# Weaving VectorE's score matmuls into ScalarE's units, with 69 instead of 74 quads on VectorE

## The chip, the cores and the metric

The kernel runs on one core of a Trainium2 chip. The metric is the device time of one execution in microseconds; lower is better. The core's engines work from their own instruction queues, in order, and wait for one another by semaphores: TensorE (PE in the profile: matrix products into PSUM, eight banks of 128 x 512 fp32), ScalarE (ACT), VectorE (DVE), GpSimd (POOL) and SyncE (SP, which mainly issues DMAs).

## The reference

One transformer block on 2048 tokens of width 640, in bf16: layer norm, attention with 32 heads of 20, a residual, a second layer norm, a gated FFN of width 1728 with the tanh Gelu, a residual. Cut to what is computed:

```python
q, k, v = split((layernorm(x) @ wqkv).reshape(B, S, 3, 32, 20))
scores  = einsum("bhqd,bhkd->bhqk", q, k) * 20 ** -0.5
o       = einsum("bhqk,bhkd->bhqd", softmax(scores), v)
h       = x + o.reshape(B, S, 640) @ wo
n       = layernorm(h)
out     = h + (gelu(n @ w_gate) * (n @ w_up)) @ w_down
```

The scores are 32 x 2048 x 2048, 134 million exponentials; they are what the kernel spends its time around.

## The kernel before

**Chunks and slots.** The queries go in eight chunks (`SIZES`, L320: 512, five of 256, two of 128). A chunk has as many slots as it takes to go through the eight groups of four heads, with 512 score columns a slot per key row: 32 slots in all. In a slot the keys are walked in key blocks of 128. A *tile* is one head's 128 x 512 scores: one matmul of 512 columns, or two of 256, or four of 128, one for each of its key blocks. A head's 20 rows sit in one of four groups of 32 rows of TensorE (`tile_position=(32 * j, 0)`, L969), so the matmuls of four different heads can run side by side. A *quad* is the four heads' tiles of one place: 16 quads a slot, 512 in all, 2048 tiles.

**Two engines take exponentials.** ScalarE takes most tiles, in *units* of three or two tiles, on PSUM banks 0 to 2 and 3 to 4 by turns, with one activation a unit that reads 1536 or 1024 columns and writes bf16 probabilities into a ring of 18 tiles (`pts` with 12 and a part of `rege` with 6, `PR, PR2`, L339). VectorE takes the quads that `D_QUADS` (L340) counts for each slot, 74 in all, with a polynomial: an eviction from PSUM to int16 for each tile (L893), then a chain of six elementwise steps for two or four tiles together, in some slots with a DMA that adds in place. `D_PART` (L341) says within what part of a slot those tiles are placed in the slots that have no lead (`lead`, L820); in the others they run ahead of their slot.

**Where VectorE's tile is issued.** At most one tile of VectorE goes with a unit (`dtile`). In slots 8 to 11 (`SIX`) it takes the unit's third bank and is part of the unit's matmuls. Elsewhere it is an operation of its own, tagged SD (L992), on a bank that is neither of the two unit sets (7, 5 or 4), priority 1, and may start once its own unit's matmuls are issued (`after=[qk]`). `fit` (L838) picks one whose row group its unit does not use.

**Sums.** Probabilities times values (`pv_op`, L926) run with four heads in four column groups into bank 6, two quads at a time in strict order; a VectorE quad is summed by itself, and the last sum of a slot stands behind all of VectorE's quads of that slot. Then VectorE copies bank 6 to `osb` (L1051), TensorE transposes it, VectorE divides. A unit's activation cannot write its ring place before the sum that read it has run.

**FFN.** When a chunk's slots are done, `post` (L1087) does output projection, residual, layer norm, gate (L1142), Gelu (in place, up to 2048 columns at once, on ScalarE), up, product (L1191) and `down` (L1222), as background between the next chunks' scores. The last chunk's has nothing left to lie behind. Each change between exponential, Gelu and square root needs a table load on ScalarE.

**The order** is not written by hand. `Sched.schedule` (L94) simulates the engines with constants for each operation's duration and picks, at each moment and engine, the ready operation of the best priority whose PSUM banks are free; TensorE's operations have a mode (row for scores, col for sums, full), and one of the current mode is preferred among the low priorities. Where TensorE would idle it inserts matmuls that compute nothing of use (`warm`, `pad`). `emit` then writes each engine's queue in the order found, with waits derived from the dependencies; on the chip the order is fixed and only the times differ. All of an operation's waits stand ahead of its first instruction, but for dependencies of TensorE on itself. Operations recorded through the helper `I` show L372 whatever they are.

Of the kernel before, what the change touches and what calls it, by code (L numbers as in the profile page):

```python
# [16 lines left out]
SEM_ANY = 0.036  # L17
# [3 lines left out]
QK_LEAD = .65  # L21
PE_AGE = 1.5
SD_ALONE = .21
P_SD = 1
LNB = 2

MODE_SWITCH = {"pe": .098, "act": 1.44}
# [19 lines left out]
class Sched:  # L47
# [3 lines left out]
    def __init__(self, nc):  # L51
        self.nc = nc
        self.ops = []
        self.lw = {}
        self.rd = {}
        self.warm = None
        self.pad = None
        self.left = {}
        self.ev = 9

    def op(self, eng, fns, dur, prio, reads=(), writes=(), acq=(), rel=(), after=(), sem=None, lat=None, mode=None, util=0.0):
        if eng == "dve" and rel and prio > self.ev:
            prio = self.ev
        o = Op()
        o.i = len(self.ops)
        o.eng, o.dur, o.lat, o.sem = eng, dur, DRAIN[eng] if lat is None else lat, sem
        o.util = util
        o.mode = mode
        o.tag = writes[0] if writes else None
        o.fns = fns if isinstance(fns, list) else [fns]  # L70
        o.prio = (prio, o.i)
        deps = set(after)
        for r in reads:
            if r in self.lw:
                deps.add(self.lw[r])
        for w in writes:
            if w in self.lw:
                deps.add(self.lw[w])
            deps.update(self.rd.get(w, ()))
        for r in reads:  # L80
            self.rd.setdefault(r, []).append(o.i)
        for w in writes:
            self.lw[w] = o.i
            self.rd[w] = []
        deps.discard(o.i)
        o.deps = deps
        o.acq = list(acq)
        o.rel = list(rel)
        o.succ = []
        o.ready = 0.0  # L90
        self.ops.append(o)
        return o.i

    def schedule(self):  # L94
        ops = self.ops
# [22 lines left out]
        while done < total:  # L118
# [4 lines left out]
            for e in ENGINES:  # L123
# [4 lines left out]
                    continue  # L128
                skipped = []
                kept = set()  # L130
                chosen = None
                while ready[e]:
                    p, i = heapq.heappop(ready[e])
                    o = ops[i]
                    got = []
                    if e == "pe" and due is not None and o.prio[0] > 0 and t < due < t + o.dur + (MODE_SWITCH[e] if mode[e] not in (None, o.mode) else 0):
                        skipped.append((p, i))
                        if len(skipped) >= 60:
                            break
                        continue  # L140
                    for bk in o.acq:
                        for b in bk.allowed:
                            if owner[b] is None and free_at[b] <= t + 1e-9 and b not in got and b not in kept:
                                got.append(b)
                                break
                        else:
                            got = None
                            break
                    if got is None:

                        if p[0] == 0:
                            kept.update(bk.allowed[0] for bk in o.acq)
                        skipped.append((p, i))
                        continue
                    skipped.append((p, i))
                    if chosen is None:
                        chosen, banks = o, got
                        if e != "pe" or p[0] < 1 or o.mode == mode[e] or t - o.ready > PE_AGE:
                            break
                    elif o.mode == mode[e]:  # L160
                        chosen, banks = o, got
                        break
                    if len(skipped) >= 60:
                        break
# [34 lines left out]
                    if chosen is None:  # L199
                        continue  # L200
                o = chosen
                if e == "pe" and o.tag and o.tag[0] == "S":
                    self.spare = self.spares[o.tag[1]]
                if e == "pe" and self.pad is not None and o.tag and o.tag[0] in ("O", "OD"):
                    s_ = o.tag[1] if o.tag[0] == "O" else o.tag[1][0]
                    self.left[s_] -= 1
                    live, begun = self.left[s_] > 0, True
                    while recent and recent[0][0] < t - PAD_WIN:
                        recent.popleft()
                    u = sum(x for _, x in recent) + o.util  # L210
                    room = due - t - MODE_SWITCH[e] if due is not None and due > t else 1e9
                    while u < PAD_MIN * PAD_WIN and o.util < 1.1 and o.dur + 0.215 < room and (live or o.tag[0] == "O"):
                        o.fns = o.fns + self.pad
                        o.dur += 0.215
                        o.util += 0.213
                        u += 0.213
                o.start = t
                if e == "act":
                    due = t + o.dur + (0.905 if o.dur > 1.2 else 1.332) - QK_LEAD if o.mode == "exp" else None
                if o.util:  # L220
                    recent.append((t, o.util))
                if o.mode is not None:
                    if o.tag and o.tag[0] == "SD" and (mode[e] != "row" or t - free[e] > 0.06):
                        o.dur = SD_ALONE
                    if mode[e] not in (None, o.mode):
                        o.dur += MODE_SWITCH[e]
                    mode[e] = o.mode
                free[e] = t + o.dur
                o.fin = t + o.dur + o.lat
                heapq.heappush(events, free[e])  # L230
                for bk in o.rel:
                    b = bk.b
                    owner[b] = None
                    free_at[b] = o.fin + SEM_LAT.get((e, "pe"), SEM_ANY)
                    last[b] = o.i
                    heapq.heappush(events, free_at[b])
                for s in o.succ:
                    q = ops[s]
                    q.ready = max(q.ready, free[e] if q.eng == e == "pe" else o.fin + SEM_LAT.get((e, q.eng), SEM_ANY))
                    q.nd -= 1  # L240
                    if q.nd == 0:
                        heapq.heappush(future[q.eng], (q.ready, q.prio, q.i))
                        heapq.heappush(events, q.ready)
                order.append(o)
                done += 1
        self.order = order
        self.span = max(o.fin for o in ops)

# [88 lines left out]
DA_ISSUE, DA_LAT = 0.95, 7.0  # L337
DA_SLOTS = (1, 2, 3, 5) + tuple(range(9, 32))
PR, PR2 = 12, 6  # L339
D_QUADS = (1,) + (2,) * 11 + (2, 3, 2, 3, 2, 2) + (3, 3, 2) * 3 + (3, 3, 2, 3, 2)  # L340
D_FIRST, D_PART = 2, 0.65  # L341
D_LEAD = ((0,) * 8, (0, 10, 20) + (36,) * 21)
D_WIDE = 18
RSQRT_MAGIC = float(0x5F3759DF)
# [6 lines left out]
def bass_sequential_preLN__mha_block__glu_gated_geglu__prompt_kernel(  # L351
# [12 lines left out]
    with ExitStack() as es:  # L364
# [120 lines left out]
        def bank(b, n=512):  # L485
            return PS[:, 512 * b.b:512 * b.b + n]
# [377 lines left out]
        d_ops = []  # L864
        exp_ops = []
        p_next = [0]

        def q_done(k):
            return sum((tuple(last_qk[c]) for c, (q0, _) in enumerate(CHUNKS) if q0 // 512 == k), ())
# [75 lines left out]
        def unit(u):  # L945
# [19 lines left out]
            def qk_mms(out, x, kk):  # L965
                s_, g, kb, j = x
                q0, nq = CHUNKS[slots[s_][0]]
                kt = kb * (512 // nq) + kk
                return lambda eng: eng.matmul(out()[:, kk * nq:(kk + 1) * nq],  # L969
                                              kt_all[32 * j:32 * j + 32, g, kt * 128:(kt + 1) * 128],  # L970
                                              qt_all[32 * j:32 * j + 32, q0 // 512, g, q0 % 512:q0 % 512 + nq],
                                              start=True, stop=True, tile_position=(32 * j, 0), skip_group_check=True)
# [7 lines left out]
            for kk in range(nkm):  # L980
                for i, x in enumerate(al):
                    if kk < 512 // CHUNKS[slots[x[0]][0]][1]:
                        fns.append(qk_mms(lambda i=i: PS[:, 512 * (s0 + i):512 * (s0 + i) + 512], x, kk))
                        reads += qk_reads(x)
            qk = op("pe", fns, 0.222, P_QK, mode="row", util=0.0533 * len(al), reads=reads, writes=[("S", u), "qkseq"] + ([("SD", xd)] if six else []), acq=bks)
            for x in al:
                last_qk[slots[x[0]][0]].append(qk)
            if six:
                bd = bks[2]
            elif xd:  # L990
                bd = Bank(*BG[tl[0][0]])
                qd = op("pe", [qk_mms(lambda: bank(bd), xd, kk) for kk in range(512 // CHUNKS[slots[xd[0]][0]][1])],  # L992
                        0.21 if xd[3] in [x[3] for x in tl] else 0.01,
                        P_SD, mode="row", util=0.0533, reads=qk_reads(xd), writes=[("SD", xd)], acq=[bd], after=[qk])
                last_qk[slots[xd[0]][0]].append(qd)
            n = 512 * na
            pk = [("P", p0 + i) for i in range(na)]
# [320 lines left out]
```

## Time and profile before

| | us |
|---|---|
| median of 3 runs | 911.2 (911.09 to 912.03) |
| the profiled execution, whole | 910.3 |
| its span, first to last instruction | 908.4 |
| first exponential starts, last one ends | 33.6, 877.3 |
| ScalarE busy from 33.6 to 877.3 | 833.1 of 843.7 |
| TensorE busy in the same stretch | 785.0 of 843.7 |
| VectorE busy in the same stretch | 727.4 of 843.7 |
| TensorE busy from 877.3 to the end | 27.6 of 31.1 |

The granted TensorE clock is full throughout. An engine's busy time is the union of its instructions' times, and two neighbouring activations overlap in the trace by some 0.2 us, so ScalarE looks busy even where one starts late: lateness has to be read from the distance of starts. In the timeline, neighbours of one kind are merged into one line: start, time from the first's start to the last's end, engine, line, shape and count, and in brackets the idle time before and what ended it.

### The profile page before, as it was taken

How to read it: one execution, taken by the hardware profiler on the slowest of the kernel's cores; microseconds unless marked ns; L12 is line 12 of the kernel's file. 1: busy time of each engine (PE TensorE's matmuls, PEld its weight loads, DVE VectorE, ACT ScalarE, POOL GpSimd, SP SyncE). 2: the span in 40 equal slices, each digit the busy share in tenths (PEclk: the TensorE clock that was granted, in tenths of full speed). 3: DMA queues.
4: the chain of work that ended last, by engine and by line, in shares of the span. 5: the costliest groups of instructions: out<-in, count | busy, mean ns of one | idle time of the engine just before them, and what ended most of it. 6: DMA issues, size and time to landing. Idle time of an engine off the chain costs nothing.

```text
span 908.4 us, 25274 instructions
## 1 busy us (share of the span) xinstructions
PE 831.5 (92%) x11183; PEld 386.0 (42%) x11228; DVE 768.4 (85%) x1445; ACT 867.3 (95%) x782; POOL 133.3 (15%) x242
## 2 busy tenths in 40 slices
PE   3999999998898887889999999999999998999998
PEld 1432232222233332334444445444444445656777
DVE  8869889988798985899987996899899889889743
ACT  7999899999999999999999999999999999999972
POOL 5001110010013110112313010021012101201200
PEclk9999999999999999999999999999999999999999
DMA  7213334344603322234444232424342343434200
GB/s 260 85 31 82 74 79 113 87 108 96 243 1 65 60 48 35 37 59 81 82 98 58 49 71 48 77 63 86 77 86 51 60 97 57 58 78 94 57 9 23
DMA packets 52933, 68.59 MB, mean 76 GB/s; under 512 B 20940, under 2 KB 38440, under 8 KB 52824
## 3 DMA queue, kind: packets, MB, share of 16 engines
q0 software_dynamic: 13392, 34.08, 20.7%
q1 hardware_dynamic: 39432, 32.89, 13.6%
q8 instruction: 88, 1.44, 0.7%
q14 instruction: 21, 0.17, 0.1%
HBM read 20.12 MB, written 8.09 MB: 31 GB/s over the span
## 4 chain that ended last, share of the span: by engine, by line
ACT 55%; PE 28%; DVE 14%; POOL 3%; issue 1%; DVEq 0%
ACT pts L372 34%; ACT rege L372 19%; PE ps L969 8%; PE ps L372 5%; PE ps L671 5%; PE ps L1142 5%; PE ps L1222 4%; DVE dwx L372 3%; DVE qt_all L372 2%; DVE rege L893 1%; DVE qt_all L893 1%; POOL nw L372 1%; DVE rege L1109 1%; ACT L372 1%; DVE stats L372 1%
## 5 line engine op out<-in xcount | busy, mean ns | idle before, releaser
L372 ACT ACTIVATE pts<-ps 128x1024 bf16<-128x1024 f32 (+1 forms) x467 | 552.9, 1330 | 7.0 <-PE ps L372 5.5
L969 PE MATMUL ps<-qt_all,kt_all 32*128 32x256 bf16 (+2 forms) x4096 | 314.2, 272 | 39.6 <-ACT pts L372 19.2
L372 ACT ACTIVATE rege<-ps 128x1024 bf16<-128x1024 f32 (+1 forms) x231 | 284.5, 1328 | 3.5 <-PE ps L372 3.1
L969 PEld LDWEIGHTS ps<-qt_all,kt_all 32*128 32x128 bf16 x4096 | 108.7, 92 | 246.2 <-ACT pts L372 124.5
L1142 PE MATMUL ps<-rege,regw 128*128 128x256 bf16 (+2 forms) x1101 | 154.5, 272 | 8.8 <-DVE rege L1191 3.6
L372 PE MATMUL ps<-pts,v_all 128*21 128x256 bf16 (+2 forms) x2330 | 122.0, 275 | 0.6 <-ACT rege L372 0.5
L1142 PEld LDWEIGHTS ps<-rege,regw 128*128 128x128 bf16 x1120 | 86.2, 98 | 59.0 <-issue 25.2
L893 DVE TENSOR_SCALAR rege<-ps 128x512 int16<-128x512 f32 x124 | 84.8, 686 | 15.6 <-PE ps L969 14.9
L372 PE MATMUL ps<-rege,v_all 128*21 128x256 bf16 (+2 forms) x1358 | 91.8, 279 | 0.7 <-DVE osb L372 0.4
L671 PE MATMUL ps<-regw 128*128 128x512 bf16 (+1 forms) x344 | 84.1, 354 | 4.7 <-ACT regw L619 1.8
L893 DVE TENSOR_SCALAR qt_all<-ps 128x512 int16<-128x512 f32 x116 | 79.4, 686 | 9.7 <-PE ps L969 8.2
L1222 PE MATMUL ps<-regw,rege 128*128 128x320 bf16 x448 | 77.6, 301 | 1.6 <-DVE rege L1226 0.5
L372 DVE TENSOR_TENSOR qt_all<-qt_all 128x1024 int16<-128x1024 f16 (+3 forms) x81 | 74.7, 922 | 1.1
L372 PEld LDWEIGHTS ps<-pts,v_all 128*21 128x21 bf16 x2330 | 53.6, 91 | 30.6 <-issue 25.0
L372 DVE TENSOR_SCALAR qt_all<-qt_all 128x2048 int16<-128x2048 int16 (+3 forms) x112 | 63.0, 566 | 0.9
L372 PE MATMUL ps<-kt_all,zer 128*32 128x512 bf16 x620 | 54.8, 386 | 0.3 <-DVE osb L372 0.3
L1191 DVE TENSOR_TENSOR rege<-rege,ps 128x512 bf16<-128x512 bf16 (+1 forms) x53 | 35.9, 679 | 21.4 <-PE ps L1142 21.0
L372 DVE TENSOR_SCALAR rege<-rege 128x1024 int16<-128x1024 int16 (+2 forms) x114 | 48.5, 439 | 5.4 <-DMA rege<-qt_all 4.3
L372 DVE TENSOR_TENSOR rege<-rege 128x1024 f16<-128x1024 f16 (+1 forms) x74 | 50.5, 683 | 0.8
L1222 PEld LDWEIGHTS ps<-regw,rege 128*128 128x128 bf16 x448 | 37.6, 98 | 28.9 <-issue 12.3
L671 PEld LDWEIGHTS ps<-regw 128*128 128x128 bf16 x360 | 28.8, 99 | 47.7 <-issue 23.8
L372 POOL DMA_DIRECT2D qt_all<-dwx x25 | 23.0, 921 | 169.2 <-DVE dwx L372 158.6
(114 smaller groups left out, 802.0 us busy)
## 6 DMA issues: line engine op xcount, KB each, us to landing
qt_all<-dwx POOLq DMA_DIRECT2D x19, 512.0 KB, 4.7
rege<-rege POOLq DMA_DIRECT2D x16, 256.0 KB, 3.6
rege<-qt_all POOLq DMA_DIRECT2D x8, 512.0 KB, 4.9
dvx<-qt_all POOLq DMA_DIRECT2D x7, 512.0 KB, 4.7
rege<-in_A_x_dram SPq DMA_DIRECT2D x5, 640.0 KB, 5.7
q_rows<-regw SPq DMA_DIRECT2D x20, 128.0 KB, 1.8
out_dram<-rege SPq DMA_DIRECT2D x16, 160.0 KB, 3.2
regw<-in_B_w_gate_dram SPq DMA_DIRECT2D x1, 2160.0 KB, 12.4
```

Source lines behind the costliest of these rows:

```text
L372: return lambda eng: getattr(eng, method)(*args, **kwargs)
L671: yield op("pe", lambda eng, l=l, r=r, k=k: eng.matmul(bank(bk, n), l, r, start=(k == 0), stop=(k == len(steps) - 1)), c_mm(n) + cold, pri ...
L893: d_ops.append(op("dve", lambda eng: eng.tensor_scalar(v[:, 512 * h:512 * h + 512], bank(b), EXP_MUL, -32000.0, ALU.mult, ALU.max), c_dve( ...
L969: return lambda eng: eng.matmul(out()[:, kk * nq:(kk + 1) * nq], kt_all[32 * j:32 * j + 32, g, kt * 128:(kt + 1) * 128], qt_all[32 * j:32 ...
L1109: op("dve", lambda eng, bk=bk, tt=tt, hf=hf, i=i: eng.tensor_tensor(h_sb[:, tt, hf * 320:(hf + 1) * 320], bank(bk, 320), h_sb[:, tt, hf * ...
L1142: op("pe", lambda eng, a=a, f=f, fi=fi: eng.matmul(bank(bk)[:, fi * nq:(fi + 1) * nq], w[:, a, F0[f]:F0[f] + 128], hnT[:, a, 128 * tb:128 ...
L1191: hdone.append(op("dve", lambda eng, bu=bu, fv=fv, w=w: eng.tensor_tensor(fv, fv, bank(bu, w), ALU.mult), c_dve(w), p, reads=[ku] + hkeys( ...
L1222: op("pe", lambda eng, f=f, o=o, hf=hf, bk=bk: eng.matmul(bank(bk, 320), ha_f[:, o:o + 128], wd[:, f, hf * 320:(hf + 1) * 320], start=(f = ...
```

## The change

Four parts. First, `JOIN`: when the planner picks a unit's score operation, it looks among the ready VectorE tiles for one whose row group the unit does not use, with as many key blocks, whose bank is free now or within 0.2 us, and which belongs to this unit or one already issued. If there is one, its matmuls are woven between the unit's, key block by key block; the unit's operation takes over its waits, and only the last matmul of the tile stays behind as the tile's own operation. The planner's start of the unit moves to when that bank is free. Second, a VectorE tile becomes ready with the unit ahead of its own (`after=[prev]`), but is held until its own unit is issued or takes it along. Third, `D_QUADS` sums to 69 instead of 74: one more in slots 12 to 17, three fewer in 18 to 26, three fewer in 27 to 31. Fourth, `D_PART` goes from 0.65 to 0.55. An SD operation that is not woven in is always counted with `SD_ALONE`.

```diff
+JOIN = 0.2
...
+                    if i in self.small and not hasattr(ops[self.small[i][2]], "start"):
+                        skipped.append((p, i))
+                        if len(skipped) >= 60:
+                            break
+                        continue
...
                 o = chosen
-                if e == "pe" and o.tag and o.tag[0] == "S":
+                t0 = t
+                if o.i in self.heads:
                     self.spare = self.spares[o.tag[1]]
+                    js, nk = self.heads[o.i]
+                    for x in sorted(x for x in ready[e] if x[1] in self.small):
+                        j, nk_, own = self.small[x[1]]
+                        q = ops[x[1]]
+                        b = next((b for b in q.acq[0].allowed if owner[b] is None and free_at[b] <= t + JOIN and b not in banks), None)
+                        if nk_ != nk or j in js or b is None or not (own == o.i or hasattr(ops[own], "start")):
+                            continue
+                        ready[e].remove(x)
+                        heapq.heapify(ready[e])
+                        q.acq[0].b = b
+                        owner[b] = q.acq[0]
+                        if last[b] is not None:
+                            q.deps = set(q.deps) | {last[b]}
+                        q.deps = set(q.deps)
+                        o.deps = set(o.deps) | (q.deps - {o.i})
+                        n = len(o.fns) // nk
+                        o.fns = sum((o.fns[n * k:n * k + n] + q.fns[k:k + 1] for k in range(nk)), [])[:-1]
+                        q.fns = q.fns[-1:]
+                        q.dur = 0.01
+                        join = q
+                        t0 = max(t, free_at[b])
+                        break
...
-                o.start = t
...
+                for o in ([o, join] if join is not None else [o]):
+                    o.start = t0 if o is chosen else free[e]
...
-                    if o.tag and o.tag[0] == "SD" and (mode[e] != "row" or t - free[e] > 0.06):
-                        o.dur = SD_ALONE
...
-D_QUADS = (1,) + (2,) * 11 + (2, 3, 2, 3, 2, 2) + (3, 3, 2) * 3 + (3, 3, 2, 3, 2)
-D_FIRST, D_PART = 2, 0.65
+D_QUADS = (1,) + (2,) * 11 + (3, 2) * 3 + (2, 2, 3) * 3 + (2,) * 5
+D_FIRST, D_PART = 2, 0.55
...
+            prev = s_last[0]
+            s_last[0] = qk
+            if not six:
+                sc.heads[qk] = (set(x[3] for x in tl), nkm) if len(set(CHUNKS[slots[x[0]][0]][1] for x in tl)) == 1 else ((0, 1, 2, 3), 0)
...
-                qd = op("pe", [qk_mms(lambda: bank(bd), xd, kk) for kk in range(512 // CHUNKS[slots[xd[0]][0]][1])],
-                        0.21 if xd[3] in [x[3] for x in tl] else 0.01,
-                        P_SD, mode="row", util=0.0533, reads=qk_reads(xd), writes=[("SD", xd)], acq=[bd], after=[qk])
+                nd = 512 // CHUNKS[slots[xd[0]][0]][1]
+                qd = op("pe", [qk_mms(lambda: bank(bd), xd, kk) for kk in range(nd)], SD_ALONE,
+                        P_SD, mode="row", util=0.0533, reads=qk_reads(xd), writes=[("SD", xd)], acq=[bd], after=[prev] if prev is not None else [])
+                sc.small[qd] = (xd[3], nd, qk)
```

More of the change, by code (lines that the diff above doesn't have):

```diff
@@ L58, in __init__ @@
         self.left = {}
+        self.heads = {}
+        self.small = {}
         self.ev = 9
@@ L130, in schedule @@
                 kept = set()
+                join = None
                 chosen = None
@@ L216, in schedule @@
                         u += 0.213
-                o.start = t
[L218 to L222, printed above, removed]
-                    if o.tag and o.tag[0] == "SD" and (mode[e] != "row" or t - free[e] > 0.06):
-                        o.dur = SD_ALONE
-                    if mode[e] not in (None, o.mode):
-                        o.dur += MODE_SWITCH[e]
-                    mode[e] = o.mode
@@ L228, in schedule @@
[L228 to L243, printed above, removed]
@@ L244, in schedule @@
-                order.append(o)
-                done += 1
+                for o in ([o, join] if join is not None else [o]):
+                    o.start = t0 if o is chosen else free[e]
+                    if e == "act":
+                        due = t + o.dur + (0.905 if o.dur > 1.2 else 1.332) - QK_LEAD if o.mode == "exp" else None
+                    if o.util:
+                        recent.append((t, o.util))
+                    if o.mode is not None:
+                        if mode[e] not in (None, o.mode):
+                            o.dur += MODE_SWITCH[e]
+                        mode[e] = o.mode
+                    free[e] = o.start + o.dur
+                    o.fin = o.start + o.dur + o.lat
+                    heapq.heappush(events, free[e])
+                    for bk in o.rel:
+                        b = bk.b
+                        owner[b] = None
+                        free_at[b] = o.fin + SEM_LAT.get((e, "pe"), SEM_ANY)
+                        last[b] = o.i
+                        heapq.heappush(events, free_at[b])
+                    for s in o.succ:
+                        q = ops[s]
+                        q.ready = max(q.ready, free[e] if q.eng == e == "pe" else o.fin + SEM_LAT.get((e, q.eng), SEM_ANY))
+                        q.nd -= 1
+                        if q.nd == 0:
+                            heapq.heappush(future[q.eng], (q.ready, q.prio, q.i))
+                            heapq.heappush(events, q.ready)
+                    order.append(o)
+                    done += 1
@@ L866, in bass_sequential_preLN__mha_block__glu_gated_geglu__prompt_kernel @@
         p_next = [0]
+        s_last = [None]
         def q_done(k):
```

## The prediction

> **What bounds the kernel now.** I read the totals of the page first, then ScalarE's instructions kept apart by shape.
>
> ```profile
> span 908.4 us, 25274 instructions
> PE 831.5 (92%) x11183; PEld 386.0 (42%) x11228; DVE 768.4 (85%) x1445; ACT 867.3 (95%) x782; POOL 133.3 (15%) x242
> ...
> L372 ACT ACTIVATE pts<-ps 128x1536 bf16<-128x1536 f32 x237 | 360.3, 1540 | 3.5 <-PE ps L372 2.2 <-PE ps L969 0.9
> L372 ACT ACTIVATE pts<-ps 128x1024 bf16<-128x1024 f32 x230 | 254.3, 1113 | 3.5 <-PE ps L372 3.3 <-PE ps L969 0.2
> L372 ACT ACTIVATE rege<-ps 128x1536 bf16<-128x1536 f32 x119 | 181.2, 1533 | 3.2 <-PE ps L372 2.9 <-PE ps L969 0.2
> L372 ACT ACTIVATE rege<-ps 128x1024 bf16<-128x1024 f32 x112 | 124.0, 1112 | 0.3 <-PE ps L372 0.3
> ```
>
> ScalarE (ACT) is the engine to watch: 698 exponentials, 356 of three tiles (1536 columns) and 342 of two (1024), with hardly any idle time before them. But neighbours overlap at their ends, so durations mislead and starts must be read. In the timeline of ScalarE alone:
>
> ```profile
> 403.45 2.49 ACT L372 ACTIVATE rege<-ps 128x1536 bf16<-128x1536 f32 x2
> 405.68 4.78 ACT L372 ACTIVATE pts<-ps 128x1536 bf16<-128x1536 f32 x4
> 410.15 2.57 ACT L372 ACTIVATE rege<-ps 128x1536 bf16<-128x1536 f32 x2
> 412.38 4.86 ACT L372 ACTIVATE pts<-ps 128x1536 bf16<-128x1536 f32 x4
> ```
>
> Four of them (two pairs) take 405.68 to 410.15, 4.47 us; a pair (five tiles) takes 2.23. Taken one by one, the usual distance to the next start is 1.330 after a three-tile one and 0.903 after a two-tile one. That floor is 356 x 1.330 + 342 x 0.903 = 782.3 us. The first starts at 33.6, the last ends at 877.3: 843.7 us, so 61.4 are something else: 37 for the Gelus inside that stretch with their table loads (the rows of 128x2048, x1536, x1792 and x1024 give 25.0, ten loads of 1.28 give 12.8, less overlap), and about 24 of lateness. Of the lateness, nine places where the exponential waits for a sum (matmuls of pts or rege with v_all) hold 10.7 us, fifty places where it waits for its own scores (L969) hold 8.9, the rest is scatter below 0.06 each. After 877.3 the chain of waits runs on TensorE (PE) almost without a break for 31.1 us: left-over FFN work and the last chunk. So the time is: 33.6, then the exponentials' floor, the Gelus, the lateness, then a TensorE tail.
>
> **How a VectorE score tile is priced today.** The score matmuls of TensorE, four lines of its timeline:
>
> ```profile
> 385.70 0.40 PE L969 MATMUL ps<-qt_all,kt_all 32*128 32x256 bf16 x6
> ...
> 387.05 0.41 PE L969 MATMUL ps<-qt_all,kt_all 32*128 32x256 bf16 x8
> ...
> 387.94 0.39 PE L969 MATMUL ps<-qt_all,kt_all 32*128 32x256 bf16 x4
> ...
> 403.69 0.61 PE L969 MATMUL ps<-qt_all,kt_all 32*128 32x256 bf16 x8
> ```
>
> x4 is a unit of two tiles, x6 at 385.70 two tiles with a VectorE tile behind them, x8 at 387.05 three with one behind: 0.39, 0.40, 0.41. A tile that follows its own unit already runs beside it, in the free 32-row group. Only where the row group is taken, or the tile stands by another unit, does it cost more (403.69: +0.22). In the built order 126 of the 259 tiles with an operation of their own follow their unit at once; 133 do not. So "issued among them" cannot save for the first half.
>
> **The change, part by part.**
> 1. *Fewer quads on VectorE.* D_QUADS sums to 69 after 74: 20 tiles move to ScalarE, and the built program has 358 three-tile and 349 two-tile exponentials: 2 x 1.330 + 7 x 0.903 = **+9.0 us**, all on ScalarE's path. Nothing hides it. VectorE, the engine that gains (20 evictions of 0.69 and five polynomial chains, some 36 us in all), was not the bound.
> 2. *Joined score matmuls.* 135 of 236 tiles are now woven in (123 into their own unit); 101 still stand apart. Counting VectorE tiles as 0.01 behind or in their own unit and 0.21 elsewhere, they cost TensorE 29.2 us before and 19.6 after. But there are nine more units (0.22 each) and 50 more changes between row, column and full mode, of about 0.11 each (PV at 403.14, sixteen matmuls worth 0.43, next scores at 403.69), +5.5. With every operation of the two built orders at the chain's prices (0.22 for a unit or a quad's sum, 0.056, 0.11 and 0.136 for full matmuls of 128, 256 and 320 columns), TensorE's work adds up to 800.5 before and 799.6 after. TensorE is not relieved. The late scores need the PE at the right moment, not less work: I give them -1.0 (bounds -5, if most of 8.9 goes, to +1).
> 3. *A wait placed in front.* A woven unit must hold VectorE's bank as well as its own before its first matmul; 107 score operations now carry a separate VectorE wait, after 30, and PE waits of this sort last 51 ns each in the trace. Before, a late VectorE stood behind the unit:
>
> ```profile
> 582.17 0.39 PE L969 MATMUL ps<-qt_all,kt_all 32*128 32x256 bf16 x2 [0.48 <-DVE rege L893]
> ```
>
> Of 153 groups with a free row group, 40 waited 0.05 to 0.85 us there, 7.6 us in all, and it hurt no exponential, whose scores were already out. Now it would: queued behind such a wait are the unit's scores, then the sums and FFN matmuls. 53 joins are with three-tile units, whose scores have only some 0.2 us of slack (start at +0.45 after the preceding two-tile exponential's start is the last that showed no lateness); with two-tile units there is 0.4 more. 53 x 40/153 x 0.19 is 2.6; with part absorbed by slack and part of the 51 ns added, **+2.3** (bounds 0 and 135 x 0.2 = 27, the planner's whole allowance; nearest to the row above, so near the low end).
> 4. *VectorE tiles earlier in a slot (0.55).* The nine waits for sums come from the ring of 18 probability tiles:
>
> ```profile
> 97.25 1.45 ACT L372 ACTIVATE rege<-ps 128x1536 bf16<-128x1536 f32 x1 [2.70 <-PE ps L372]
> ```
>
> At a slot's end its last sum waits for VectorE's tiles of that slot, the ring stays full, ScalarE waits. In the built order these are the places where a unit's ring space is freed by a sum that TensorE issues after that unit's scores: nine such before, the nine found in the trace, five after. A place with nothing but the sum between cost 0.38 to 0.69 (mean 0.56), one with another unit between 1.29 to 2.92. After: two of the first kind, three of the second (2.0, 2.5 and 1.3 by likeness): 6.9 instead of 10.7, **-3.8** (bounds -8 and 0).
> 5. *The end.* After the last scores 51 fewer down matmuls (320 columns, 0.136 each by the chain) and 36 more gate/up ones (0.056) are left, but one Gelu of 1792 columns, before ahead of the last exponentials, now stands behind them, between two more table loads. ScalarE's path before that point loses 1.68. In the tail:
>
> ```profile
> 877.33 1.28 ACT L372 ACT_TABLE_LOAD   x1
> 878.62 0.20 ACT L372 ACTIVATE nm<-off 128x1 f32<-128x1 f32 x1
> 881.27 0.70 ACT L619 ACTIVATE rege<-ps 128x640 bf16<-128x640 bf16 x1 [2.44 <-PE ps L613]
> ```
>
> The copy at 881.27 (3.94 behind the last exponential) comes at 1.28 + 0.20 + 1.28 + 1.68 = 4.44: 0.5 later. The second new load falls in the 4.23 idle before the square root. From the copy: output projection 1.36, then 59 ups and 23 downs 6.4 (before: 4.0), second transposes and copy 1.2, 140 gate/ups 7.8, VectorE 0.5, 28 downs 4.0, add and store 2.8: 29.4 against 31.1, **-1.7** (bounds -3.5, +2.5). Gelu and tail together -3.4.
>
> The trace has a Gelu starting 1.30 us after its load does (857.51, 858.81), so 1.28 is a load's whole price. ScalarE: Activation LUTs in the Trainium skill, section What ACT_TABLE_LOAD costs, adds a drain of 1.38 us, 2.66 in all; by it the copy would come 2.8 us later still and the sum would be +5.9. The trace disagrees, so it gets no chance of its own.
>
> **Sum.** 9.0 - 1.0 + 2.3 - 3.8 - 3.4 = +3.1 us against the profiled execution (span 908.4, 910.3 as a whole). The median of the runs shown is 0.9 above it, 911.2, and goes with it: **914.3**.
>
> **Rivals.** About 0.2% (1.8 us) is what a measurement here can tell from no change.
> - *Lateness nearly gone, faster.* The woven order removes both kinds: ring -7, scores -5, no new waits: 9.0 - 12 - 3.4 = -6.4, 904.8. For it: VectorE has 36 us less to do, and over-full pairs of units (more PE work between scores than the exponentials last) fall from 244 to 220. Against: PE work is the same, and five ring places are visible in the order. Chance 0.27.
> - *VectorE in front of the scores, much slower.* If half of the 135 joined units wait 0.2 and the slack is already used up by PE being busy, +10 in place of 2.3, about 922. It decides from a mean of some 0.15 us in three-tile units. For: VectorE's 85% and the 40 waits above. Against: VectorE gets lighter. Chance 0.15. In TensorE: Matmul & The Clock Gate of the Trainium skill, section The mechanism, matmuls start and end strictly in program order; that is the rule that lets one bank hold up a unit, and the line at 582.17, where the sums stood behind it, agrees.
> - *It does nothing that matters:* weaving saves nothing as half ran side by side, and ring and tail pay for the nine units: -1 to +1, 911.3. Chance 0.13.
> - *Forecast:* 0.45, its own range 912 to 918.
>
> Faster 0.28, same 0.14, slower 0.58. The range 904.5 to 921 holds the forecast, the small case, most of the faster one and half of the slower.
>
> **What would show it.** ScalarE: 707 exponentials at the same 1.330 and 0.903; lateness by sums near 7 us at five places; the last Gelu behind the last exponential, with the tail near 29.4. TensorE: 4 tiles in 0.41, more VectorE releases ahead of L1001. I am wrong if lateness falls below 13 us in all (faster), or if waits for scores rise far above 10 us.

## The result, and the profile after

The changed kernel takes 914.5 us (median of 12 runs, 911.3 to 915.9), the kernel before 911.1 on the same chip (median of 12): a ratio of 1.0034, 95% interval 1.0024 to 1.0045. It is slower by 3.4 us. The totals of its page:

```profile
span 912.2 us, 25442 instructions
PE 840.6 (92%) x11261; PEld 380.1 (42%) x11261; DVE 739.8 (81%) x1405; ACT 876.6 (96%) x793; POOL 125.1 (14%) x238
```

And ScalarE's exponentials apart by shape (busy time and mean; then idle time before them, by what ended it):

```profile
L403 ACT ACTIVATE pts<-ps 128x1536 bf16<-128x1536 f32 x238 | 378.9, 1607 | 6.8 <-PE ps L403 3.7 <-PE ps L1001 3.0
L403 ACT ACTIVATE pts<-ps 128x1024 bf16<-128x1024 f32 x236 | 276.1, 1186 | 0.1
L403 ACT ACTIVATE rege<-ps 128x1536 bf16<-128x1536 f32 x120 | 192.3, 1612 | 3.7 <-PE ps L403 2.2 <-PE ps L1001 1.5
L403 ACT ACTIVATE rege<-ps 128x1024 bf16<-128x1024 f32 x113 | 134.4, 1192 | 0.0
```

VectorE fell from 768.4 to 739.8 us of work, ScalarE rose from 867.3 to 876.6, and there are 707 exponentials in place of 698. The span is best taken apart along ScalarE, with the starts: the first exponential, then all exponentials at 1.330 and 0.903 us each (the floor), then what the distances between neighbouring exponentials exceed that (lateness, by what was waited for; the rest is scatter below 0.06 each), then everything else up to the table load behind the last exponential (Gelus, loads), then the tail. The same sum for every kernel of this study, each from its own profiled execution, in us:

| | span | first | floor | late: sums | late: scores | scatter | Gelus, loads | tail |
|---|---|---|---|---|---|---|---|---|
| before | 908.4 | 33.6 | 782.3 | 10.7 (9 places) | 8.8 | 2.8 | 39.0 | 31.0 |
| after | 912.2 | 32.9 | 791.3 | 7.0 (5) | 9.5 | 3.4 | 37.9 | 30.4 |
| e1, quads alone | 913.0 | 33.8 | 791.3 | 7.0 (6) | 9.6 | 3.3 | 37.5 | 30.4 |
| e2, 0.55 alone | 903.4 | 33.5 | 782.3 | 6.2 (7) | 8.3 | 3.0 | 39.0 | 31.1 |
| e3, both numbers | 910.5 | 33.6 | 791.3 | 2.6 (4) | 11.9 | 3.3 | 37.4 | 30.5 |
| e4, tile behind | 913.4 | 33.6 | 791.3 | 7.0 (5) | 9.2 | 4.1 | 37.8 | 30.3 |
| e5, transposes 4.0 | 907.2 | 32.7 | 791.3 | 6.8 (5) | 4.7 | 3.5 | 37.8 | 30.3 |
| e6, no weaving | 913.8 | 32.4 | 791.3 | 7.2 (5) | 4.6 | 3.4 | 37.7 | 37.3 |
| e7, 0.50 alone | 908.8 | 33.1 | 782.3 | 6.1 (6) | 14.1 | 3.3 | 38.9 | 31.0 |
| e8, price 0.21 | 916.2 | 32.7 | 791.3 | 7.5 (4) | 5.1 | 4.0 | 37.7 | 37.9 |
| e9, planner alone | 924.8 | 33.7 | 782.3 | 7.4 (5) | 8.7 | 3.4 | 31.1 | 58.1 |

(The prediction put the lateness before at about 24 and the Gelus at 37: there the last exponential ahead of each table load was counted with the first.)

After against before: floor +9.0, sums -3.7, scores +0.7, scatter +0.6, Gelus -1.1, tail -0.6, first -0.7; rounded like this they add up to 4.2, and the two spans differ by 3.8. The scores are where the inside differs from the sum. Of the 9.5 us, 5.3 lie in one hole from 802 to 813. TensorE's and ScalarE's timeline there, and the transfer of the layer-normed tokens:

```profile
799.85 4.37 SPq L403 DMA_TRANSPOSE rege<-o_nat  x2
...
801.51 0.63 PE L1001 MATMUL ps<-qt_all,kt_all 32*128 32x128 bf16 x24 [0.65 <-DVE qt_all L925]
801.95 2.37 ACT L403 ACTIVATE rege<-ps 128x1536 bf16<-128x1536 f32 x2 [0.30 <-PE ps L1001]
...
803.49 0.40 PE L1001 MATMUL ps<-qt_all,kt_all 32*128 32x128 bf16 x12
...
804.20 2.38 ACT L403 ACTIVATE pts<-ps 128x1536 bf16<-128x1536 f32 x2
804.38 0.40 PE L1001 MATMUL ps<-qt_all,kt_all 32*128 32x128 bf16 x8
...
808.47 0.72 PE L1179 MATMUL ps<-rege,regw 128*128 128x256 bf16 x5 [3.70 <-DMA rege<-o_nat]
809.12 0.40 PE L1001 MATMUL ps<-qt_all,kt_all 32*128 32x128 bf16 x16
...
809.57 2.53 ACT L403 ACTIVATE pts<-ps 128x1536 bf16<-128x1536 f32 x2 [2.99 <-PE ps L1001]
...
813.34 1.45 ACT L403 ACTIVATE rege<-ps 128x1536 bf16<-128x1536 f32 x1 [1.25 <-PE ps L1001]
```

Three things come together there. First, the unit at 801.51 is a woven one. It waits 0.65 us until VectorE has emptied the bank of its woven tile, and its exponential at 801.95 starts 0.6 late. Second, the planner put an FFN gate matmul (L1179) ahead of the next scores, counting that a DMA transpose lands 2.8 us after its issue of 1.25. The two transposes issued here took 8.0 and 6.3 us from issue to landing, the second until 808.4. TensorE stood 3.7 us, and the exponential behind it started 3.1 late. Third, the clock that TensorE was granted fell to half 1 us behind that wait. The windows view of the wait and of the 3.4 us at half clock (length; TensorE's busy time and count; granted clock; DMA share, GB/s):

```profile
804.78:808.47 3.69, 0.00 (x0) 1.00 0.93 178
809.45:812.86 3.41, 3.41 (x56) 0.50 0.46 87
```

The exponential at 813.34 is another 1.4 late, behind scores made at half clock. Outside this hole late scores are 4.2 us, half of before. The line at 809.12 also shows weaving as such: sixteen matmuls of 128 columns, three tiles of ScalarE and one of VectorE, in 0.40, which is what twelve take at 803.49 (0.40).

### The profile page after: what moved, and what is told of

It reads as the page before. It is cut to its first block, busy times and chain, and to the rows that moved or that the text cites. A ratio compares the mean times of both kernels' runs of the same rounds, so it can differ in the third digit from the quotient of the medians.

```text
span 912.2 us, 25442 instructions
## 1 busy us (share of the span) xinstructions
PE 840.6 (92%) x11261; PEld 380.1 (42%) x11261; DVE 739.8 (81%) x1405; ACT 876.6 (96%) x793; POOL 125.1 (14%) x238
## 4 chain that ended last, share of the span: by engine, by line
ACT 84%; PE 13%; DVE 2%; DMA 1%; POOL 1%; issue 0%
ACT pts L403 52%; ACT rege L403 29%; PE ps L702 4%; PE ps L1001 3%; PE ps L403 2%; ACT L403 2%; PE ps L1179 1%; PE ps L1259 1%; DMA rege<-o_nat 1%; PE ps L644 0%; ACT qt_all L403 0%; ACT regw L650 0%; ACT v_all L403 0%; POOL nw L403 0%; DVE rege L1228 0%
## 5 line engine op out<-in xcount | busy, mean ns | idle before, releaser
L403 ACT ACTIVATE pts<-ps 128x1536 bf16<-128x1536 f32 (+1 forms) x474 | 566.9, 1397 | 6.9 <-PE ps L403 3.7
L1001 PE MATMUL ps<-qt_all,kt_all 32*128 32x256 bf16 (+2 forms) x4096 | 307.5, 273 | 35.4 <-ACT pts L403 17.7
L403 ACT ACTIVATE rege<-ps 128x1536 bf16<-128x1536 f32 (+1 forms) x233 | 296.8, 1408 | 3.7 <-PE ps L403 2.2
L1001 PEld LDWEIGHTS ps<-qt_all,kt_all 32*128 32x128 bf16 x4096 | 103.0, 92 | 249.6 <-ACT pts L403 130.9
L1179 PE MATMUL ps<-rege,regw 128*128 128x256 bf16 (+2 forms) x1120 | 161.5, 275 | 12.6 <-ACT rege L403 5.1
L1179 PEld LDWEIGHTS ps<-rege,regw 128*128 128x128 bf16 x1120 | 85.3, 98 | 67.1 <-issue 32.9
L925 DVE TENSOR_SCALAR qt_all<-ps 128x512 int16<-128x512 f32 x104 | 71.0, 685 | 21.1 <-PE ps L1001 20.6
L1259 PE MATMUL ps<-regw,rege 128*128 128x320 bf16 x448 | 82.3, 302 | 1.5 <-DVE sd L403 0.5
L403 DVE TENSOR_TENSOR qt_all<-qt_all 128x1024 int16<-128x1024 f16 (+3 forms) x77 | 68.7, 892 | 1.1
L403 DVE TENSOR_SCALAR qt_all<-qt_all 128x2048 int16<-128x2048 int16 (+3 forms) x106 | 58.1, 550 | 5.3 <-DMA qt_all<-qt_all 4.0
L925 DVE TENSOR_SCALAR dvx<-ps 128x512 int16<-128x512 f32 x52 | 35.7, 686 | 14.3 <-PE ps L1001 14.0
```

Source lines behind the costliest of these rows:

```text
L403: return lambda eng: getattr(eng, method)(*args, **kwargs)
L925: d_ops.append(op("dve", lambda eng: eng.tensor_scalar(v[:, 512 * h:512 * h + 512], bank(b), EXP_MUL, -32000.0, ALU.mult, ALU.max), c_dve( ...
L1179: op("pe", lambda eng, a=a, f=f, fi=fi: eng.matmul(bank(bk)[:, fi * nq:(fi + 1) * nq], w[:, a, F0[f]:F0[f] + 128], hnT[:, a, 128 * tb:128 ...
L1259: op("pe", lambda eng, f=f, o=o, hf=hf, bk=bk: eng.matmul(bank(bk, 320), ha_f[:, o:o + 128], wd[:, f, hf * 320:(hf + 1) * 320], start=(f = ...
```

## The experiments

Each was run beside the kernel before on the same chip; ratios are to that, with 95% intervals.

**e1: the quads alone.**

```diff
-D_QUADS = (1,) + (2,) * 11 + (2, 3, 2, 3, 2, 2) + (3, 3, 2) * 3 + (3, 3, 2, 3, 2)
+D_QUADS = (1,) + (2,) * 11 + (3, 2) * 3 + (2, 2, 3) * 3 + (2,) * 5
```

> The kernel before with the new D_QUADS alone (0.65, old planner). Theory (ScalarE's floor pays, weaving is worth nothing): floor 791.3 us (+9.0); the waits for sums lose the three late places of before (534.7, 618.7, 642.8, 3.6 us); the last Gelu falls behind the last exponential here too, -2.5; scores as late as before, 8.9. About 914. Rival (weaving earns its keep): 917 or more, as the lateness that the changed kernel saved at the scores (some 4 us outside one hole at 805 to 813) is not saved here.

915.4 us, 1.0051 (1.0035 to 1.0067), against some 914 expected. The floor rises by 9.0, the three late places are gone (7.0 of sums is left), the Gelu slips into the tail. The rival's bound of 917 was not reached. Against the kernel before, the quads alone cost 4.5 us.

**e2: `D_PART` 0.55 alone.**

```diff
-D_FIRST, D_PART = 2, 0.65
+D_FIRST, D_PART = 2, 0.55
```

> The kernel before with D_PART 0.55 alone. Theory: same floor 782.3; the places where an exponential waits for a sum fall from nine to seven, the one of 2.9 us at 97 among those gone; 911.1 - 3.5, about 907.6, clearly faster than before. Rival (the ring is relieved by weaving or by fewer quads, not by where VectorE's tiles lie): within 1 us of 911.

905.8 us, 0.9947 (0.9932 to 0.9963): faster than both kernels, by 5.2 us than the one before, and 1.8 below what was expected. ScalarE's timeline around 97 us, the kernel before first, then this one:

```profile
89.86 4.69 ACT L372 ACTIVATE pts<-ps 128x1536 bf16<-128x1536 f32 x4
97.25 2.37 ACT L372 ACTIVATE rege<-ps 128x1536 bf16<-128x1536 f32 x2 [2.70 <-PE ps L372]
```

```profile
93.14 2.50 ACT L372 ACTIVATE rege<-ps 128x1536 bf16<-128x1536 f32 x2
95.37 4.79 ACT L372 ACTIVATE pts<-ps 128x1536 bf16<-128x1536 f32 x4
```

The four exponentials from 89.86 should hand over at 94.33 and do so at 97.25; here the hand-over at 95.37 comes 2.23 after two exponentials, which is the floor. The table has sums 4.5 us earlier and nothing else moved by more than 0.5.

**e3: both numbers, the planner of before.**

> The kernel before with both numbers of the change and without its planner, so nothing is woven. Theory: floor 791.3, waits for sums at about four places and 3 us, Gelu and tail -2.5, scores 8.9: 911.1 + 9.0 - 7.7 - 2.5, about 910 to 912, no slower than the changed kernel. Rival (weaving earns its keep): slower than the changed kernel, 916 or more.

911.2 us, 1.0000 (0.9988 to 1.0012): within the theory's 910 to 912, and level with the kernel before. So the two numbers together cost nothing, and all of the 3.4 us comes with the new planner. The profiled execution was 1.5 us above the median. Two stretches of 3.4 us with the granted clock at one half lie in it (from 677.7 and 834.7), with 2.7 of its 11.9 us of late scores in and just behind them.

**e4: the order of the changed kernel, with the joined tile behind its unit.** In the block that joins, the dependencies and the weaving are left out; the planned order stays as it is, operation for operation.

```diff
-                        o.deps = set(o.deps) | (q.deps - {o.i})
-                        n = len(o.fns) // nk
-                        o.fns = sum((o.fns[n * k:n * k + n] + q.fns[k:k + 1] for k in range(nk)), [])[:-1]
-                        q.fns = q.fns[-1:]
```

> The changed kernel with exactly its order of operations, but the joined tile's matmuls stand behind the unit's and its wait for VectorE stands there too. Theory: 135 tiles run in a free row group either way; few of the waits are long; within 1 us of the changed kernel, 914.5. Rival A (waits in front of the scores cost): at least 2 us faster, 912.5 or less. Rival B (weaving key block by key block saves TensorE time): at least 2 us slower, 916.5 or more.

915.3 us, 1.0052 (1.0037 to 1.0067), within 1 us of the changed kernel's 914.5, and their intervals overlap. Neither rival: the waits moved ahead of the scores cost nothing that the time shows, and the interleaving itself saves nothing that the time shows. The tail is 30.3 here too, and TensorE waits 3.1 us for the DMA transpose in the same hole, with the granted clock at one half from 807.8 for 6.8 us. In this trace five of the 124 joined tiles start more than 0.05 us after their unit's last matmul does, 0.8 us in all, and 0.45 of that is the tile whose wait made one exponential 0.6 late in the changed kernel (801.95): so little had the moved waits to cost. What joining does for the time here, it does through the planner's count.

**e5: the hole taken away.** The changed kernel with the landing of a DMA transpose counted at 4.0:

```diff
-        sem=f"xp{wkey[1]}", lat=2.8, after=after)
+        sem=f"xp{wkey[1]}", lat=4.0, after=after)
```

> The changed kernel with one planner constant altered: the landing of a DMA transpose is counted with 4.0 us, not 2.8. It still has 707 units and about the same places where sums come late. Theory (the 5.3 us of late scores between 802 and 813 come from an FFN gate matmul that stands ahead of the scores and waits 3.7 us for a DMA transpose): that hole goes, 914.5 - 4.5, about 910. Rival (the planner's new order costs time all over): within 1 us of 914.5.

909.7 us, 0.9987 (0.9977 to 0.9996). Late scores fall from 9.5 to 4.7 us, and no other term moves by more than 0.2. ScalarE's timeline in the same place is now without a gap:

```profile
801.46 2.37 ACT L403 ACTIVATE rege<-ps 128x1536 bf16<-128x1536 f32 x2 [0.21 <-PE ps L1001]
803.71 4.64 ACT L403 ACTIVATE pts<-ps 128x1536 bf16<-128x1536 f32 x4
808.19 2.41 ACT L403 ACTIVATE rege<-ps 128x1536 bf16<-128x1536 f32 x2
```

So that hole was what made the change slower rather than level. The half clock went with it: the mean granted clock was below full in each of the 12 executions of the changed kernel (0.996 or 0.998) and in all five of e4, and in three of ten here; of 35 executions of the kernel before, 21 were at full clock.

**e6: the changed kernel without any joining.**

```diff
-                        if nk_ != nk or j in js or b is None or not (own == o.i or hasattr(ops[own], "start")):
+                        if True or nk_ != nk or j in js or b is None or not (own == o.i or hasattr(ops[own], "start")):
```

> The changed kernel with its numbers and its other planner edits, but no tile is ever joined to a unit. Theory: the waits for sums stay near 7 us, since the two largest early places (units 6/7 and 52/53) stand in this order too; small score lateness goes back up from 4 to 9 or 12 us; the tail is longer, as 32.0 us of matmuls stand behind the last scores and not 23.7: 916 to 920. Rival (weaving and its waits are what made the changed kernel slower): 912 or less.

916.7 us, 1.0057 (1.0039 to 1.0075), in the range expected, but only half for the reason given. Sums stay at 7.2, and the tail grows to 37.3. Late scores did not go back up: 4.6 us. Joining has no part in those. The stretch behind the last exponential in the windows view, this kernel and then the changed one (length; busy time and count of PE, weight loads, VectorE, ScalarE; GpSimd; clock, DMA):

```profile
876.50:913.80 37.30, 33.10 (x407) 27.01 (x404) 15.38 (x36) 10.99 (x14) 0.00 (x0) 1.00 0.05 19
```

```profile
881.90:912.20 30.30, 25.16 (x333) 20.14 (x330) 11.61 (x30) 10.91 (x14) 0.00 (x0) 0.99 0.03 12
```

74 more matmuls, 7.9 us of TensorE, stand in the tail. The exponentials end 5.4 us earlier, as this order has no hole, and the tail takes it back.

**e7: `D_PART` 0.50 alone.**

> The kernel before with D_PART 0.5 alone. Theory: the place at 150 us (1.3) goes as well, compared with 0.55: 905.8 - 1, about 905, and faster than both kernels. Rival (VectorE's tiles now run so early that its evictions hold up scores): 907 or more.

907.4 us, 0.9956 (0.9939 to 0.9972). The place at 150 us does not stand in its order, but at 0.55 it had already cost only 0.06 (e2, at 144 us), so there was next to nothing left to gain: sums are 6.1, against 6.2. Late scores are 14.1 in its profile, most of the excess at 808 to 841 us, far from the slots that `D_PART` touches; 3.4 of it lies in and just behind a stretch of 6.8 us with the granted clock at one half, from 833.7 (that execution, 910.8 us as a whole, was 3.4 above the median, so its terms overstate). Faster than before, not told apart from 0.55; the expected extra microsecond did not come.

**e8: the planner's price.** The kernel before with both new numbers and one constant.

```diff
-                        0.21 if xd[3] in [x[3] for x in tl] else 0.01,
+                        SD_ALONE,
```

> The kernel before with the two new numbers and one more constant: every VectorE tile with an operation of its own is planned at 0.21 us, never at 0.01. Nothing is woven. Theory (the planner's price of a tile, not the weaving, set the small score lateness, the two early places at units 6/7 and 52/53, and the work left to the tail): waits for sums near 7, late scores about 5, tail about 36, as without weaving in the changed planner: 914 to 918. Rival (the new readiness rule of the tiles did it): late scores 9 to 12, tail about 31, near the 911 of the same numbers with the old price.

918.9 us, 1.0094 (1.0068 to 1.0120), 7.7 more than e3, which differs in this constant alone. It was expected 914 to 918. Late scores fall from 11.9 (9.1 without the stretches at half clock) to 5.1, sums rise from 2.6 to 7.5, the tail goes from 30.5 to 37.9: every feature of the new planner but the joining. The early place shows best. ScalarE in e3, and then here:

```profile
38.06 2.40 ACT L372 ACTIVATE rege<-ps 128x1536 bf16<-128x1536 f32 x2
40.98 4.62 ACT L372 ACTIVATE pts<-ps 128x1536 bf16<-128x1536 f32 x4 [0.52 <-PE ps L372]
```

```profile
37.14 2.40 ACT L372 ACTIVATE rege<-ps 128x1536 bf16<-128x1536 f32 x2
44.03 2.37 ACT L372 ACTIVATE pts<-ps 128x1536 bf16<-128x1536 f32 x2 [4.49 <-PE ps L372]
```

Two exponentials last 2.23 from start to start; the third starts 0.69 late in e3 and 4.66 late here. In the changed kernel the same place costs 2.65 (42.24 instead of 39.59).

**e9: the new planner alone,** with 74 quads and 0.65.

> The changed planner, weaving included, with the numbers of before (74 quads, 0.65). Theory: floor 782.3 again (9.0 less), lateness 15 to 16, but 51.5 us of matmuls stand behind the last scores and not 23.7, with two Gelus there: the tail grows from 30 to about 58, 925 to 929, much slower than both. Rival (weaving relieves TensorE, so that 74 quads are better with it): at most 908.

926.4 us, 1.0165 (1.0148 to 1.0182), as expected. The floor is the low one, the exponentials end at 866.6, earliest of all, and TensorE then has 53.6 us left to do:

```profile
866.60:924.80 58.20, 53.58 (x603) 43.90 (x604) 27.45 (x58) 14.20 (x16) 2.59 (x14) 0.99 0.09 27
```

With this planner and the old numbers the FFN is pushed out behind the attention. The new numbers bring it back under the exponentials, and the 69 quads cost 9.0 us of ScalarE. Which of the two numbers brings it back is not shown: with 74 quads and 0.55 the new planner finds no order at all, and 69 quads with 0.65 were not tried with it.

## Why the prediction was right, point by point

The forecast was 914.3 and slower; 914.5 was measured. The sum holds, and several terms hold with it. Two were wrong and met the measured value together by chance, and the one for the end was twice too large.

1. *Fewer quads, +9.0 on ScalarE's path.* Right to the tenth: 358 and 349 exponentials, at the same 1.330 and 0.903. e1 and e3 show the same floor. Nothing hid it.
2. *Joining does not relieve TensorE.* Right. e4 undoes it at a fixed order and the time stays. But the late scores got -1.0, where 4.6 went away outside the hole, by the planner's changed price (e8: 9.1 to 5.1 with that constant alone, half-clock stretches left out). That edit stood in the diff, as the price of a tile that is not joined, and I left it out of the sum.
3. *Waits in front of the scores, +2.3.* The wait is real and the size is wrong. One exponential starts 0.6 late for it (801.95), and taking all such waits away (e4) gains nothing. The row I counted from, 40 waits among 153 groups, is 5 among 124 in e4. It was of a kernel whose VectorE had more to do (768.4 us against 739.8) and whose planner did not choose its pairs by the bank; which of these made the difference was not tried. The counts of joins were a little off too: the order that the kernel builds joins 124 tiles, 50 of them with three-tile units, not 135 and 53. Behind the wait at 582.17, which the prediction shows, stood four filler matmuls and the next unit's scores, not the sums that it names. The much slower rival falls with the term. What filled its place was something I had no row for: two DMA transposes of 8.0 and 6.3 us under an FFN matmul that stands ahead of scores, and the half clock behind that wait (+4.7 together; e5). Terms 2 and 3 together, +1.3, met +0.7 by chance.
4. *The ring, -3.8.* Measured -3.7, at the five places that the order of the program shows, with 2.65, 0.46, 2.11, 0.50 and 1.26 against 2.0, 0.56, 2.5, 0.56 and 1.3 in the forecast. I gave the gain to 0.55 alone. It is more than that: 0.55 alone takes 4.5 and the quads alone 3.7, both together 8.1 (e1, e2, e3), and the new price gives 4.9 back at the early places (e8).
5. *Gelu and tail, -3.4.* Mis-sized: -1.1 and -0.6. The copy came where it was put, 4.4 behind the last exponential. The missing 1.7 us are the Gelu's (it took only 1.1 off, not 1.7) and TensorE's: eleven up matmuls, beyond the 59 that were counted, stand ahead of the output projection and wait for the Gelu until 886.46, and the down block at 892.58 waits 0.52 for VectorE. (The parts listed behind the copy add up to 24.1; with the 4.44 and the copy's own 0.7 that is 29.2, not quite the 29.4 stated.) The table load:

```profile
883.19 0.20 ACT L403 ACTIVATE nm<-off 128x1 f32<-128x1 f32 x1
883.41 1.28 ACT L403 ACT_TABLE_LOAD   x1
884.71 1.70 ACT L403 ACTIVATE rege<-rege 128x1792 bf16<-128x1792 bf16 x1
```

The Gelu starts 1.30 after its load starts. The 2.66 us that the Trainium skill gives for a switch (ScalarE: Activation LUTs, What ACT_TABLE_LOAD costs) is again not what this trace shows.

Of the rivals, the one that wanted lateness nearly gone is half the case without the hole: the same kernel then stands at 909.7 (e5), 1.8 us below before, with late scores 4.1 lower, where the rival had 5, and sums 3.9 lower, where it had 7. The rival that nothing matters describes e3, where the ring (-8.1) and the Gelu and tail (-2.1) pay for the nine units; in the changed kernel the new price gives part of the ring's gain back.

## What to carry to other kernels

Before paying to run something in parallel, look whether it already does: half of the tiles ran in a free row group behind their unit for 0.01 us, and weaving gained nothing on the chip. In a kernel whose order a planner writes, a constant is part of the change: raising one tile's price from 0.01 to 0.21 moved 7 us of FFN work into the tail, and what joining did for the time was to lower that price again. Look at what an in-order engine waits for ahead of the work that feeds the bound engine: one wait of 3.7 us there, with the half clock behind it, cost 4.7. Test the parts of a bundled change one by one; here one number of the four edits was worth 5.2 us alone, and the rest of the bundle hid it.

## What the runs showed of the hardware that was not expected

A DMA transpose of 128 x 640 bf16 took 2.6 to 8.0 us from issue to landing within one execution (26 of them, median 2.9 in the changed kernel, 2.7 to 3.8 over the kernels here); TensorE's FFN waited 3.7 us for one in the changed kernel, 3.1 in e4, 0.8 to 1.0 in e1 and e3, and in the others not more than 0.3. While the changed kernel waited, its DMA engines were busy for 0.93 of the time, against 0.34 from the first exponential to the last. Why some transposes are slow was not tried.

The granted TensorE clock fell to half for 3.4 or 6.8 us in four of the profiled executions before their last exponential: in the changed kernel and e4 around that wait of TensorE (from 809.45 and 807.82), in e3 (677.7 and 834.7) and e7 (833.7) without a wait of that length. Exponentials start late in and behind these stretches, by 1.5 us behind the wait in the changed kernel, 2.7 in e3 and 3.4 in e7. That the wait brings the half clock on is likely but not shown: none of the 17 executions of the two kernels whose traces have it was at full clock throughout, and seven of ten without it (e5) were. What brings it on in the other kernels stays open.
